# Cosine attention with a highway layer: k scaled ahead of the product, transfers over 128 lanes

## The chip, the cores and the metric

The kernel runs on one core of a Trainium2 chip. The metric is the device time of one execution in microseconds. The core has a matrix engine (TensorE, PE in the profile; its weight loads are listed apart as PEld), three engines for element-wise work (VectorE or DVE, ScalarE or ACT, GpSimd or POOL), and SyncE (SP), which here only issues transfers. Every engine works through its own list of instructions in order, and semaphores hold an instruction back until what it needs is there. Transfers are issued from SP, ACT and POOL and run on the core's 16 DMA engines.

## The reference

Eight batches b of 12 heads, 448 positions and 64 numbers a head; q, k and v are float32. Then a gated layer on all 3584 rows of 768 numbers:

```python
def _attn_ref(q, k, v, tau):                 # (8, 12, 448, 64), tau = 0.1
    q_n = q / (np.linalg.norm(q, axis=-1, keepdims=True) + 1e-06)
    k_n = k / (np.linalg.norm(k, axis=-1, keepdims=True) + 1e-06)
    scores = np.matmul(q_n, k_n.transpose(0, 1, 3, 2)) / tau
    scores = scores - np.max(scores, axis=-1, keepdims=True)
    attn = np.exp(scores)
    attn = attn / (np.sum(attn, axis=-1, keepdims=True) + 1e-09)
    return np.matmul(attn, v)

def _moe_ref(x, w_h, w_t, b_t):              # x: (3584, 768), weights 768 x 768
    H = np.maximum(x @ w_h, 0.0)
    T = 1.0 / (1.0 + np.exp(-(x @ w_t + b_t)))
    return T * H + (1.0 - T) * x
```

The rows of x are the positions of a batch, its columns the 12 heads side by side.

## The kernel before, in words

**Attention.** The heads of a batch go in six pairs p: head p in lanes 0 to 63 and head p + 6 in lanes 64 to 127 once they are transposed. A group g holds two pairs. Of the 448 keys of a head, 384 are three blocks c of 128; the last 64 keys of both heads of a pair make one more block, the tail ("t" in names). For each batch the kernel does the following:

- Squares on ACT (L353 q, L376 k, L387 k's tail, L373 k of batch 0), sums over 64 numbers on DVE (L361, L382, L389), and seven small steps of Newton's method on DVE (L401 to L408) that turn a sum of squares n into 1/sqrt(n), held in y. The factor 1/tau is folded into the norm of q.
- Scaling of q by its own y (L419), one multiplication of 128x448 for each of two halves t and three groups. It runs on POOL, but for one of batch 0 on DVE.
- k is not scaled. DVE copies it into pair order as float16 (kc, L471; for batch 0 the casts ck, L465), and POOL casts its tail (kb, L479).
- Transposes on PE with an identity as the moving operand (q: L431; k: L450 and L452), and copies out of PSUM on DVE (qT: L436, kT: L458).
- Scores on PE (L508, L519), 448 queries wide. Six exponentials of a pair on ACT (L514) and one of the tail (L521) write E and Et as float16; the scale of the exponential is y of the key, one number a lane. No maximum is subtracted: a cosine over tau is at most 10.
- Products with v on PE (L533, L538, L546); a column of ones in v gives the sum of the exponentials. DVE takes its reciprocal (L553) and scales (L554) into x.

**The gated layer.** The rows of a batch are cut into four parts i, numbered g = 4b + i; three have 128 rows (two rows j of each of 64 lanes) and the fourth has 64. PE transposes x (L577), DVE copies (L579), PE multiplies with wt and wh (L593, L590), DVE adds the bias into z (L602), ACT takes a tanh with the constant scale 0.5 (L609), DVE makes the gate (L611), relu(H) - x (L605) and their product hm (L614), POOL adds x (L619) into one of four output buffers os, and SP stores it (L628; the fourth part L626).

**Transfers.** SP loads q, the tails of k and v, and the bias, and stores. POOL loads k, v and the weights with a cast to float16. ACT issues three loads at the start. q of a batch is loaded as two transfers of 64 lanes, s = 0 and 1 (L284, L287); an output of 128 rows is stored as two transfers of 64 lanes, h = 0 and 1.

**Order.** The order is written out. Every operation has a number, in the order in which the Python code names it, and ORDER is a permutation of all 1,879 numbers. Each engine gets its instructions in that order. SLOTS says for each tile which of its ring's buffers it uses. Nothing is planned when the kernel is built. A change of the operations so comes with a new ORDER and new SLOTS.

Of the kernel before, what the change touches and what calls it, by code (L numbers as in the profile page):

```python
# [92 lines left out]
""".split()  # L93
)

SLOTS = {
    "qr": "01010101",
    "kr": "0120120",
    "kt": "01010010",
    "kb": "01010101",  # L100
    "kp": "01010101",
    "vr": "01010101",
    "vt": "01010110",
    "vp": "01010101",
    "sq": "0120210120202120120120102120120120101102202101020",
# [89 lines left out]
def kernel(  # L195
# [436 lines left out]
    for b in range(B):  # L632
        if b == 0:
# [5 lines left out]
            for p in range(2, 6):  # L639
                ld_k0(p, "SP")  # L640
# [97 lines left out]
```

## Time and profile before

| what | value |
|---|---|
| median of 3 runs | 289.96 us (289.58 to 292.29) |
| the profiled execution | 289.78 us, of which the profile's span is 288.0 |
| granted TensorE clock | 0.995 |
| busy: PE / DVE / ACT / POOL | 255.9 / 241.1 / 242.5 / 130.3 us |
| exponentials (L514, L521) | 336 instructions, 195.1 us busy |
| moved by DMA | 38.63 MB in 51,251 packets |
| of this SP's queue (q1) | 26.35 MB in 24,976 packets |

Instructions of one engine overlap: the next starts before the last has ended. So a group's busy time divided by its count is longer than the distance of two starts, and the distance is what an instruction costs in a full queue. A "DMA share" is the mean busy share of the 16 DMA engines; packets of several queues can overlap on one engine, so a share over 1 is possible. Idle time of an engine is put down to what ended it.

### The profile page before, as it was taken

The numbers are of one execution on the slowest core, as the hardware profiler recorded it, in microseconds if no ns is written. First come the engines' busy times: TensorE is split into PE (matmuls) and PEld (weight loads), VectorE is DVE, ScalarE is ACT, GpSimd is POOL, SyncE is SP. The second block draws the span as 40 slices with busy tenths as digits, with TensorE's granted clock in tenths as the row PEclk, the third lists the DMA queues.
The fourth block names the chain that finished last, engine by engine and source line by source line (L and its number), as shares of the span: only waits on it lengthen the run. The fifth ranks groups of instructions, "written<-read, shape, count | busy, mean of one in ns | idle before, by whom it ended". The sixth has DMA issues, their size and how long they took to land.

```text
span 288.0 us, 7655 instructions
## 1 busy us (share of the span) xinstructions
PE 255.9 (89%) x3024; PEld 160.7 (56%) x3024; DVE 241.1 (84%) x544; ACT 242.5 (84%) x421; POOL 130.3 (45%) x166
## 2 busy tenths in 40 slices
PE   0156899999999999999999999999999999999991
PEld 0122556655655656565756575665755576656650
DVE  2896895479999899999979999799999878565994
ACT  3378999999799989999999997989999787894220
POOL 1659048113574629034945168070764091206260
PEclk9999999999999999999999999999999999999997
DMA  7999999999498696822879917758004606000636
GB/s 174 231 218 227 258 236 204 231 196 141 56 102 146 113 226 186 180 68 35 108 141 238 145 31 192 165 81 168 2 3 112 81 3 192 2 2 2 191 88 185
DMA packets 51251, 38.63 MB, mean 134 GB/s; under 512 B 37648, under 2 KB 48016, under 8 KB 51216
## 3 DMA queue, kind: packets, MB, share of 16 engines
q1 hardware_dynamic: 24976, 26.35, 38.4%
q0 software_dynamic: 24896, 11.21, 31.6%
q10 hardware_dynamic: 1344, 0.59, 1.0%
q8 instruction: 23, 0.38, 0.5%
q14 instruction: 12, 0.10, 0.1%
HBM read 38.34 MB, written 11.01 MB: 171 GB/s over the span
## 4 chain that ended last, share of the span: by engine, by line
PE 38%; ACT 35%; DMA 8%; DVE 8%; issue 4%; SPq 2%; POOL 2%; POOLq 0%; ACTq 0%; DVEq 0%
ACT E L514 25%; PE B L593 15%; PE B L508 5%; PE B L538 5%; DMA qr<-in_q_dram 5%; ACT Et L521 5%; PE B L590 3%; DMA kt<-in_k_dram 2%; PE B L546 2%; ACT sq L353 2%; ACT tt L609 2%; POOL os L619 2%; PE B L533 2%; PE B L431 2%; PE B L577 1%
## 5 line engine op out<-in xcount | busy, mean ns | idle before, releaser
L514 ACT ACTIVATE E<-B,y 128x448 f16<-128x448 f32 x288 | 163.2, 690 | 12.3 <-PE B L508 12.0
L619 POOL TENSOR_TENSOR os<-x,hm 128x384 f32<-128x384 f16 x53 | 48.6, 929 | 87.3 <-DVE hm L614 60.6
L593 PEld LDWEIGHTS <-xT 128*128 128x128 f16 x576 | 52.1, 97 | 36.6 <-issue 7.6
L419 POOL TENSOR_TENSOR qn<-qr,y 128x448 f16<-128x448 f32 x47 | 44.3, 960 | 49.8 <-DVE y L408 30.7
L593 PE MATMUL B<-wt,xT 128*128 128x384 f16 x288 | 57.6, 326 | 0.7 <-DVE xT L579 0.3
L593 PE MATMUL B<-wh,xT 128*128 128x384 f16 x288 | 57.3, 326 | 0.8 <-ACT E L514 0.3
L508 PE MATMUL B<-qT,kT 64*128 64x448 f16 x288 | 49.3, 369 | 6.6 <-ACT Et L521 2.3
L538 PE MATMUL B<-vp,E 128*128 128x65 f16 x864 | 44.9, 194 | 0.1
L538 PEld LDWEIGHTS <-E 128*128 128x128 f16 x864 | 39.1, 98 | 4.0 <-issue 0.4
L609 ACT ACTIVATE tt<-z 128x768 f16<-128x768 f32 (+1 forms) x32 | 25.4, 798 | 16.9 <-DVE z L602 16.9
L605 DVE SCALAR_TENSOR_TENSOR hm<-B,x 128x384 f16<-128x384 f32 x56 | 29.9, 547 | 5.8 <-PE B L593 3.7
L533 PE MATMUL B<-vp,Et 128*128 128x130 f16 x144 | 32.3, 224 | 0.5 <-ACT Et L521 0.2
L602 DVE TENSOR_TENSOR z<-B,bias 128x384 f32<-128x384 f32 x48 | 26.1, 548 | 7.5 <-PE B L593 4.7
L521 ACT ACTIVATE Et<-B,y 128x448 f16<-128x448 f32 x48 | 31.9, 686 | 0.1
L554 DVE SCALAR_TENSOR_TENSOR x<-B,rd 128x448 f16<-128x448 f32 x48 | 29.3, 617 | 0.8
L361 DVE TENSOR_REDUCE n<-sq 128x14 f32<-128x896 f32 (+1 forms) x25 | 25.7, 1034 | 0.9 <-ACT sq L353 0.9
L353 ACT ACTIVATE sq<-qr 128x896 f32<-128x896 f32 (+1 forms) x24 | 23.3, 977 | 3.1 <-DMA qr<-in_q_dram 3.1
L508 PEld LDWEIGHTS <-kT 64*128 64x128 f16 x288 | 11.9, 95 | 25.0 <-issue 16.0
L450 PE MATMUL B<-ident,kp 128*128 128x128 f16 x144 | 14.7, 230 | 11.1 <-POOL ident masks.py:199 10.1
L382 DVE TENSOR_REDUCE n<-sq 128x18 f32<-128x1152 f32 (+2 forms) x17 | 21.5, 1270 | 0.8 <-ACT sq L376 0.8
L450 PEld LDWEIGHTS <-kp 128*128 128x128 f16 x144 | 10.5, 101 | 16.8 <-issue 10.0
L458 DVE COPY kT<-B 128x1024 f16<-128x1024 f16 (+1 forms) x27 | 16.6, 619 | 2.8 <-PE B L452 2.8
(53 smaller groups left out, 356.4 us busy)
## 6 DMA issues: line engine op xcount, KB each, us to landing
qr<-in_q_dram SPq DMA_DIRECT2D x14, 672.0 KB, 9.2
out_dram<-os SPq DMA_DIRECT2D x48, 192.0 KB, 3.1
kr<-in_k_dram POOLq DMA_DIRECT2D x7, 576.0 KB, 9.7
vr<-in_v_dram POOLq DMA_DIRECT2D x7, 576.0 KB, 8.8
vt<-in_v_dram SPq DMA_DIRECT2D x16, 96.0 KB, 7.4
out_dram<-os SPq DMA_DIRECT2D x16, 96.0 KB, 2.3
qr<-in_q_dram SPq DMA_DIRECT2D x6, 224.0 KB, 5.3
kt<-in_k_dram SPq DMA_DIRECT2D x14, 96.0 KB, 7.4
```

What stands on the lines that cost most here:

```text
L353: nc.scalar.activation(dst(), src(), AF.Square, scale=tau)
L419: ENG[eng].tensor_mul(R("qn", 3 * b + g)[:, :, t, :], R("qr", b)[:, g + 3 * t, :].rearrange("l (j d) -> l j d", d=D), R("y", b)[:, c : c + ...
L508: nc.tensor.matmul(R("B", ("S", n, c, t))[:, 0:S], lhsT=R("kT", i)[ln, s, 128 * c : 128 * c + 128], rhs=R("qT", i)[ln, s, :], start=True, ...
L514: nc.scalar.activation(R("E", n)[:, at : at + 7, :].rearrange("l j x -> l (j x)"), R("B", ("S", n, c, t))[:, 0:S], AF.Exp, scale=R("y", b) ...
L521: op("ACT", f"expt {n}", lambda: nc.scalar.activation(R("Et", n).rearrange("l j x -> l (j x)"), R("B", ("St", n))[:, 0:S], AF.Exp, scale=R ...
L533: nc.tensor.matmul(U[:, 2 * c : 2 * c + 2, :], lhsT=Et[:, 2 * c : 2 * c + 2, :].rearrange("l j x -> l (j x)"), rhs=vp[:, 6:8, 0:65], start ...
L538: nc.tensor.matmul(U[:, 2 * c + t, :], lhsT=E[:, at : at + 2, :].rearrange("l j x -> l (j x)"), rhs=vp[:, 3 * t + m, 0:65], start=False, s ...
L554: op("DVE", f"ev {n}", lambda: nc.vector.scalar_tensor_tensor(out=R("x", b)[:, :, D * p : D * p + D], in0=U_()[:, :, 0:D], scalar=0.0, in1 ...
L593: nc.tensor.matmul(P[:, 0:MH], lhsT=xT[:, cc, :], rhs=w_[:, cc, MH * mh : MH * mh + MH], start=(cc == 0), stop=(cc == CC - 1))
L605: op("DVE", f"hm {g} {mh}", lambda at=at, sl=sl, mh=mh: nc.vector.scalar_tensor_tensor(out=R("hm", g)[:, sl], in0=R("B", at)[:, 0:MH], sca ...
L609: op("ACT", f"th{nb} {g}", lambda: nc.scalar.activation(R("tt", g)[:, 0:W], R("z", g)[:, 0:W], AF.Tanh, scale=0.5), r=[("z", g)], w=[("tt" ...
L619: op(eng, f"out {g} {mh}", lambda sl=sl, mh=mh: ENG[eng].tensor_add(R("os", g)[:, sl], xpart(mh), R("hm", g)[:, sl]), r=[("gg", g), ("x", ...
```

## The change

- k is multiplied by its own y before it is transposed (scale_k, "kn"): one multiplication of 128x384 a pair, on DVE for the first two pairs of batch 0 and on POOL for the other 46. They take the place of the copies kc and the casts ck. The cast of k's tail becomes a multiplication too (scale_kb). The buffer kp now holds one pair and has six places.
- The exponentials have no scale from y any more.
- k's transposes of a group go into one PSUM tile; for batch 0 they come in three operations, with three copies.
- q of a batch, or a group of it in batch 0, is one transfer of 128 lanes, and so is the store of an output of 128 rows. The fourth part of a batch is stored as before.
- 18 products of zeros, 128x128 by 128x512, run on PE before its first real work.
- In batch 0 the loads of k and of its tail, but for the first, are issued by SP, and the norms of the first q and k share one Newton chain.
- ORDER and SLOTS are new. Among SP's instructions the first store stood behind the first half of q's load of batch 4, and now stands ahead of that load.

```diff
+    WARM = 18
-        kp=(2, [128, NP, NC, 2, D], FP16),
+        kp=(6, [128, NC, 2, D], FP16),
+    op("DVE", "zw", zero("DVE", [(wz[:, :], 0.0)]), w=[("wz",)])
+    for i in range(WARM):
+        op("PE", f"wm {i}", lambda i=i: nc.tensor.matmul(R("B", ("W", i))[:, :], lhsT=wz[:, 0:128], rhs=wz[:, 128:640],
+                                                         start=True, stop=True), r=[("wz",)], w=[("B", ("W", i)), ("wm",)], mode="F")
-    def q_src(b, s):
-        return q[b].rearrange("(u s) (l j) d -> s l u (j d)", s=2, j=NJ)[s]
+    def q_src(b):
+        return q[b].rearrange("(u s) (l j) d -> s l u (j d)", s=2, j=NJ)
...
-        for s in range(2):
-            def fn(s=s):
-                d, a = R("qr", b)[64 * s : 64 * s + 64], q_src(b, s)
...
+        def fn():
+            d, a = R("qr", b), q_src(b)
+            if len(gs) == 3:
+                ENG[eng].dma_start(d[:, :, :], a)
...
+    def kcol(b, p):
+        return R("y", b)[:, KCS[b > 0][0][p] : KCS[b > 0][0][p] + 6].rearrange("l (t c) -> l t c", t=2).unsqueeze(3).to_broadcast([128, 2, NC, D])
...
+    def scale_k(b, p, eng):
+        def fn():
+            if b == 0:
+                a = R("os", ("f0", p // 2)).rearrange("l (i h c d) -> l i h c d", i=2, h=2, c=NC)[:, p % 2]
+            else:
+                a = R("kr", b)[:, p::6, :].rearrange("l h (c d) -> l h c d", c=NC)
+            ENG[eng].tensor_mul(R("kp", 6 * b + p).rearrange("l c t d -> l t c d"), a, kcol(b, p))
...
-                ENG[eng].tensor_copy(R("kb", b)[ln, :, ab, :], R("kt", b)[ln, :, :])
+                ENG[eng].tensor_mul(R("kb", b)[ln, :, ab, :], R("kt", b)[ln, :, :],
+                                    R("y", b)[ln, c : c + 6].unsqueeze(2).to_broadcast([64, NP, D]))
...
-                                         AF.Exp, scale=R("y", b)[:, col : col + 1])
+                                         AF.Exp)
...
-            for h in range(2):
-                if tail:
+            if tail:
+                for h in range(2):
                     nc.sync.dma_start(rows[6, :, MH * h : MH * h + MH], O[64 * h : 64 * h + 64, 0:MH])
-                else:
-                    nc.sync.dma_start(rows[2 * i + h], O[64 * h : 64 * h + 64, :])
+            else:
+                nc.sync.dma_start(rows[2 * i : 2 * i + 2], O[:, :])
```

More of the change, by code (lines that the diff above doesn't have):

```diff
@@ L98 @@
     "kr": "0120120",
-    "kt": "01010010",
+    "kt": "01010101",
     "kb": "01010101",
-    "kp": "01010101",
+    "kp": "012345102345012345012345012345021345021345021435",
     "vr": "01010101",
-    "vt": "01010110",
+    "vt": "01010010",
     "vp": "01010101",
-    "sq": "0120210120202120120120102120120120101102202101020",
+    "sq": "0121012012012012012012101201212120120201201210211",
     "n2": "01010101",
     "y": "01201201",
-    "tu": "0110100101010",
+    "tu": "010101010101",
     "qn": "012012012012012012012012",
@@ new lines @@
+    "z": "01010101010101010010101010011010",
+    "tt": "01010110010110100101100101100101",
+    "hm": "01201021012010210201210120101201",
+    "os": "01230123212032030103021031303102310",
+    "B": (
+        "0123456701234567012456701347036512602371065021403450146234671350264371632047236450123740612736025743"
+        "1204573516372450130264731657240315035103521074503624735370462140563175406175203461753753146201736107"
+        "5234057642130542160574362513650274607267014325615261432065370624306574120712347605641340715260431524"
+        "7253627104527630254163410653217402712470631246071352130436714250361745304703516402761254607327465203"
+        "1546123567421362047260752414076542076351023174503720614537247325410623745103762401765367254176215604"
+        "1376410753620136725430215346126703517015436702531426714507361235467013475026714307162457130264"
@@ L279, in ld_q @@
     def ld_q(b, gs=range(3), eng="SP"):
-        for s in range(2):
-            def fn(s=s):
-                d, a = R("qr", b)[64 * s : 64 * s + 64], q_src(b, s)
-                if len(gs) == 3:
-                    ENG[eng].dma_start(d, a)
-                else:
-                    g = gs[0]
-                    ENG[eng].dma_start(d[:, g::3, :], a[:, g::3, :])
-            op(eng, f"ldq {b} {gs[0]} {s}", fn, w=[("qr", b, g) for g in gs])
+        def fn():
[3 more added lines that the diff above has]
+            else:
+                ENG[eng].dma_start(d[:, gs[0] :: 3, :], a[:, :, gs[0] :: 3, :])
+        op(eng, f"ldq {b} {gs[0]}", fn, w=[("qr", b, g) for g in gs])
     def ld_k0(p, eng):
@@ L437, in turn_q, with turn_k @@
             op("DVE", f"cpq{parts} {b} {g} {s}", cp, r=[("B", ("Tq", i))], w=[("qT", i, s)] if s is not None else [("qT", i, 0), ("qT", i, 1)])
-    def turn_k(b, g, joint):
+    def turn_k(b, g):
         i = 3 * b + g
-        for s in (None,) if joint else range(2):
-            at = ("Tk", i, s)
-            ss = range(2) if joint else (s,)
-            def fn(at=at, ss=ss):
-                T = R16(at)
-                for n, s in enumerate(ss):
-                    p = 2 * g + s
-                    for c in range(NC):
-                        nc.tensor.transpose(T[:, 512 * n + 128 * c : 512 * n + 128 * c + 128],
-                                            R("kp", b)[:, p, c].rearrange("l t d -> l (t d)"), ident[:, :])
-                    nc.tensor.transpose(T[:, 512 * n + 384 : 512 * n + 512],
-                                        R("kb", b)[:, p].rearrange("l ab d -> l (ab d)"), ident[:, :])
-            op("PE", f"tk{len(ss)} {b} {g} {s}", fn, r=[("kp", b, 2 * g + s_) for s_ in ss] + [("kb", b), ("id",)],
-               w=[("B", at)], mode="F")
-            def cp(at=at, ss=ss):
-                nc.vector.tensor_copy(R("kT", i)[:, ss[0] : ss[-1] + 1].rearrange("p s x -> p (s x)"), R16(at)[:, 0 : 512 * len(ss)])
-            op("DVE", f"cpk{len(ss)} {b} {g} {s}", cp, r=[("B", at)], w=[("kT", i, s_) for s_ in ss])
@@ L461, in cast_k0 @@
-    def cast_k0(p, eng):
-        def fn():
-            a = R("os", ("f0", p // 2)).rearrange("l (i h x) -> l i h x", i=2, h=2)[:, p % 2]
-            a, d = a.rearrange("l h (c d) -> l h c d", c=NC), R("kp", 0)[:, p].rearrange("l c t d -> l t c d")
-            ENG[eng].copy(d, a) if eng == "ACT" else ENG[eng].tensor_copy(d, a)
-        op(eng, f"ck {p}", fn, r=[("os", ("f0", p // 2), p)], w=[("kp", 0, p)])
-    def copy_k(b):
-        for t in range(2):
-            def fn(t=t):
-                nc.vector.tensor_copy(R("kp", b).rearrange("l p c t d -> l (p c) t d")[:, :, t],
-                                      R("kr", b)[:, 6 * t : 6 * t + 6, :].rearrange("l p (c d) -> l (p c) d", c=NC))
-            op("DVE", f"kc {b} {t}", fn, r=[("kr", b, p) for p in range(NP)], w=[("kp", b, p) for p in range(NP)])
@@ L475, in cast_kb, with part, tails @@
-    def cast_kb(b, eng):
+        at = ("Tk", i)
+        def part(s):
+            for c in range(NC):
+                nc.tensor.transpose(R16(at)[:, 512 * s + 128 * c : 512 * s + 128 * c + 128],
+                                    R("kp", 6 * b + 2 * g + s).rearrange("l c t d -> l c (t d)")[:, c], ident[:, :])
+        def tails():
+            for s in range(2):
+                nc.tensor.transpose(R16(at)[:, 512 * s + 384 : 512 * s + 512],
+                                    R("kb", b)[:, 2 * g + s].rearrange("l ab d -> l (ab d)"), ident[:, :])
@@ new lines, in copy @@
+        def copy(lo, n):
+            d = R("kT", i)
+            if lo == 0:
+                nc.vector.tensor_copy(d.rearrange("p s x -> p (s x)")[:, :], R16(at)[:, :])
+            elif n == 384:
+                nc.vector.tensor_copy(d[:, (lo - 1) // 2, 0:384], R16(at)[:, 256 * (lo - 1) : 256 * (lo - 1) + 384])
+            else:
+                nc.vector.tensor_copy(d[:, :, 384:512], R16(at).rearrange("p (s x) -> p s x", s=2)[:, :, 384:512])
+        if b > 0:
+            op("PE", f"tk8 {b} {g}", lambda: (part(0), part(1), tails()),
+               r=[("kp", 6 * b + 2 * g), ("kp", 6 * b + 2 * g + 1), ("kb", b), ("id",)], w=[("B", at)], mode="F")
+            op("DVE", f"cpk1024 {b} {g}", lambda: copy(0, 1024), r=[("B", at)], w=[("kT", i, 0), ("kT", i, 1), ("kT", i, "t")])
+            return
@@ new lines, in turn_k @@
+        for s in range(2):
+            op("PE", f"tk3 {b} {g} {s}", lambda s=s: part(s), r=[("kp", 6 * b + 2 * g + s), ("id",)] + ([("wm",)] if g == 0 and s == 0 else []),
+               w=[("B", ("Tk", i), s)], mode="F")
+            op("DVE", f"cpk384 {b} {g} {s}", lambda s=s: copy(1 + 2 * s, 384), r=[("B", at, s)], w=[("kT", i, s)])
+        op("PE", f"tk2 {b} {g}", tails, r=[("kb", b), ("id",)], w=[("B", ("Tk", i), "t")], mode="F")
+        op("DVE", f"cpk256 {b} {g}", lambda: copy(1, 256), r=[("B", at, "t")], w=[("kT", i, "t")])
@@ L502, in scores @@
         n = 6 * b + p
-        KC, KT = KCS[b > 0]
         for c in range(NC):
@@ L512, in fe @@
                 def fe(c=c, t=t):
-                    at, col = 7 * (2 * c + t), KC[p] + 3 * t + c
+                    at = 7 * (2 * c + t)
                     nc.scalar.activation(R("E", n)[:, at : at + 7, :].rearrange("l j x -> l (j x)"), R("B", ("S", n, c, t))[:, 0:S],
-                                         AF.Exp, scale=R("y", b)[:, col : col + 1])
-                op("ACT", f"exp {n} {c} {t}", fe, r=[("B", ("S", n, c, t)), ("y", b, "k", p)], w=[("E", n)])
+                                         AF.Exp)
+                op("ACT", f"exp {n} {c} {t}", fe, r=[("B", ("S", n, c, t))], w=[("E", n)])
         def ft():
             nc.tensor.matmul(R("B", ("St", n))[:, 0:S], lhsT=R("kT", i)[:, s, 384:512], rhs=R("qT", i)[:, s, :], start=True, stop=True)
-        op("PE", f"qkt {n}", ft, r=[("qT", i, s), ("kT", i, s)], w=[("B", ("St", n))], mode="F")
+        op("PE", f"qkt {n}", ft, r=[("qT", i, s), ("kT", i, "t")], w=[("B", ("St", n))], mode="F")
         op("ACT", f"expt {n}", lambda: nc.scalar.activation(
-            R("Et", n).rearrange("l j x -> l (j x)"), R("B", ("St", n))[:, 0:S], AF.Exp,
-            scale=R("y", b)[:, KT + p : KT + p + 1]), r=[("B", ("St", n)), ("y", b, "t")], w=[("Et", n)])
+            R("Et", n).rearrange("l j x -> l (j x)"), R("B", ("St", n))[:, 0:S], AF.Exp),
+           r=[("B", ("St", n))], w=[("Et", n)])
     def attend(b, p):
@@ L635 @@
             ld_k0(0, "ACT")
-            ld_kt(0, "ACT")
-            ld_k0(1, "ACT")
+            ld_kt(0, "SP")
+            for p in range(1, 6):
+                ld_k0(p, "SP")
             ld_q(0, [1], "SP")
-            for p in range(2, 6):
-                ld_k0(p, "SP")
             ld_q(0, [2], "SP")
@@ L659 @@
             newton(0, 66, 84, [("k", 3), ("k", 4), ("k", 5)])
-            for p in range(NP):
-                cast_k0(p, "DVE")
         else:
@@ L679 @@
                 newton(b, 0, 84, [("q", g) for g in range(3)] + [("k", p) for p in range(6)] + [("t",)])
-            copy_k(b)
-        cast_kb(b, "POOL")
+        scale_kb(b, "POOL")
         if b == 0:
@@ L690 @@
             scale_q(b, g, ("DVE", "POOL") if first else ("POOL", "POOL"))
+            for s in range(2):
+                scale_k(b, 2 * g + s, "DVE" if first else "POOL")
             turn_q(b, g, 2 if first else 1)
-            turn_k(b, g, b > 0)
+            turn_k(b, g)
         for p in range(NP):
```

39 lines of the change are left out of this document (16 added, 23 removed), and 145 rows, old and new, of the table ORDER.

## The prediction

> **What bounds the kernel now.** I read the head of the page first, then busy time by stage, then single rows of ACT for the spacing of its instructions, then the transfers, since the change touches all of these.
>
> From the page (busy time; DMA queue 1; the chain that ended last; groups):
>
> ```profile
> PE 255.9 (89%) x3024; PEld 160.7 (56%) x3024; DVE 241.1 (84%) x544; ACT 242.5 (84%) x421; POOL 130.3 (45%) x166
> ...
> q1 hardware_dynamic: 24976, 26.35, 38.4%
> ...
> PE 38%; ACT 35%; DMA 8%; DVE 8%; issue 4%; SPq 2%; POOL 2%; POOLq 0%; ACTq 0%; DVEq 0%
> ...
> L514 ACT ACTIVATE E<-B,y 128x448 f16<-128x448 f32 x288 | 163.2, 690 | 12.3 <-PE B L508 12.0
> L619 POOL TENSOR_TENSOR os<-x,hm 128x384 f32<-128x384 f16 x53 | 48.6, 929 | 87.3 <-DVE hm L614 60.6
> ...
> L419 POOL TENSOR_TENSOR qn<-qr,y 128x448 f16<-128x448 f32 x47 | 44.3, 960 | 49.8 <-DVE y L408 30.7
> ...
> out_dram<-os SPq DMA_DIRECT2D x48, 192.0 KB, 3.1
> ```
>
> Three engines are nearly full and the chain changes between PE and ACT. By stage (columns: stage, its length, then busy us of PE, PEld, DVE, ACT, POOL, each with its count, then the granted clock, DMA share, GB/s):
>
> ```profile
> 60.00:100.00 40.00, 39.15 (x427) 23.48 (x426) 37.90 (x76) 38.21 (x64) 21.34 (x25) 1.00 0.88 120
> 100.00:140.00 40.00, 38.81 (x501) 24.62 (x500) 38.09 (x83) 38.89 (x69) 17.27 (x20) 1.00 0.71 141
> 140.00:180.00 40.00, 39.24 (x496) 25.30 (x493) 37.30 (x80) 37.41 (x66) 23.21 (x27) 1.00 0.77 141
> ```
>
> In the middle ACT is idle 1 to 3 of 40 us and DVE 2 to 3; POOL has half its time free. No single engine can be relieved alone for more than a few per cent. Now ACT's rows in order of time:
>
> ```profile
> 39.93 5.88 ACT L514 ACTIVATE E<-B,y 128x448 f16<-128x448 f32 x11
> 45.62 0.71 ACT L521 ACTIVATE Et<-B,y 128x448 f16<-128x448 f32 x1
> ...
> 97.72 0.98 ACT L609 ACTIVATE tt<-z 128x768 f16<-128x768 f32 x1
> 98.45 0.77 ACT L521 ACTIVATE Et<-B,y 128x448 f16<-128x448 f32 x1
> 98.97 1.31 ACT L376 ACTIVATE sq<-kr 128x1152 f32<-128x1152 f16 x1
> 100.02 1.31 ACT L514 ACTIVATE E<-B,y 128x448 f16<-128x448 f32 x2
> ```
>
> Starts, not durations, give the price of an instruction in a full queue: eleven exponentials take 45.62 - 39.93 = 5.69 us, 0.517 each; the tanh with a constant scale over 768 columns takes 0.73, the square over 1152 takes 1.05. The last two give 0.32 / 384 = 0.83 ns a column and 0.09 us fixed.
>
> The SP queue:
>
> ```profile
> SPq L628 <- POOL os L619: 104.5, 11, 23.0
> ...
> 92.36 8.21 SPq L628 DMA_DIRECT2D out_dram<-os  x4
> ```
>
> The first store leaves at 92.36 us, and SP spends 104.5 us waiting for outputs to store: today neither its issue time nor the 3.1 us landing of a store is on the path.
>
> **The change part by part.**
>
> *Constant scale in the exponentials.* By the line above, 448 columns with a constant scale would take 0.09 + 0.37 = 0.46 us against 0.517. Times 336 (288 + 48) that is 19 us less on ACT; at the other end 0, if the spacing belongs to reading PSUM. I take 19, since both constant-scale rows lie on the line. The Trainium skill, "ScalarE: Activation LUTs", section "What ACT_TABLE_LOAD costs", prices one [128,1] pointer operand at about 93 ns; by it the sum would be 31 us, where these rows bear out about 60 ns each. DVE and PE are then late next: DVE sheds the copies of k (L471, 14 of 551 ns, 7.7 us) and the casts (L465, 6 of 494 ns, 3.0), and gains two scalings (1.2) and a few smaller copies of kT, about 9 us net. I count 11 us of gain on the path, with 0 and 19 as ends.
>
> *k scaled on POOL.* 46 multiplications of 128x384. The trace has none; the nearest rows are L419 (960 ns for 448 columns, 0.82 us scaled) and L619 (0.93 us for 384): 38 to 43 us. The 16 casts of k's tail become two-input products, 0.54 to about 0.82 us: 4 us. POOL goes from 130 to about 175 of 288 us. Cover: its idle time ahead of L619 and L419, 87.3 + 49.8 us. The new wait is k's transposes for POOL; behind them on PE stand the scores, and ACT waits for those. PE waits today 7 us in all for q's scaling; I take 0 more for k's, between 0 and 20 (a wait of up to 10 us for hm stands ahead of a scaling in POOL's queue, twice over the run).
>
> *q as one transfer, stores as one.* SP issues 10 loads of q in place of 20 and 24 stores in place of 48: 34 issues of 0.6 us off a queue that waits 104.5 us; 0 on the path, but 1 us at the start, where eight issues stand ahead of a q load in the chain. Before, the first store stood behind a load of q (batch 4) that waits for its buffer; in the new order it stands ahead of it, so it leaves when its last sum on POOL is done: 77.9 us in the trace, less 4 for faster exponentials, 74 us.
>
> What matters is the shape of the new store. q's load stays 128 x 6 x 448 on both sides, as its two strides run into one. The store's output does not: two rows j of a group lie 768 elements apart and the 64 lanes 5376, so the changed program carries 2 x 64 x 768 against 128 x 768. Its outermost count falls from 64 to 2. How are transfers dealt to the sixteen DMA engines? The trace answers for the old ones. SP's 121 issues carry 23,040 pieces (for instance 48 stores x 64, 14 loads of q x 64 x 6); the page counts 24,976 packets, and 24,976 - 23,040 = 1,936 = 121 x 16, one closing packet for every engine and issue. All those have outermost counts of 64 or 128 and inner ones of 1 to 6. An issue of 64 pieces (store) and one of 384 (q) take the same 0.60 and 0.62 us, so SP hands over a shape, not a list of pieces. A shape is cut along a dimension, and with the inner counts at 2, 3 or 6 the only one that gave sixteen parts was the outermost. With an outermost count of 2 that leaves **two engines**. No row shows such a case; the other end is sixteen, as now.
>
> The Trainium skill says the same for this case: "DMA: Bandwidth & Descriptors", section "Why a DMA increments its semaphore by 16 and not by 1", takes the largest number up to 16 that divides the slowest dimension of both sides, and on SP's queue always the lowest-numbered engines. By it the 24 stores all use the same two. The trace agrees for 64 and 128; for 2 no run here shows it.
>
> Price: a store is 128 pieces of 3,072 bytes. The trace's quicker half of such packets took 121 to 134 ns, so 64 in a row take 7.7 us on an engine, against some 1.5 us today. The stage from 279.50 to 286.00, mostly stores, moves 199 GB/s at a DMA share of 0.72, 17.3 GB/s an engine or 11.4 us a store: the upper end, as sixteen engines then disturb each other. I take 7.7: 24 x 7.7 = 186 us on each of the two engines. After 74 us they also carry their sixteenth of the rest: about 27 us of SP's own packets, in line behind the stores, and 37 of POOL's loads (packets at their quickest, 18 to 74 ns and 49 ns). Queues overlap on an engine, since the DMA share reaches 1.26 in one stage; I count half of POOL's, 19.
>
> Sum: 74 + 186 + 27 + 19 = 306. The pair is not always fed (four output buffers; loads wait behind stores), 10 us; the profiled execution lies 1.8 us over its span, 289.78 against 288.0, and 0.2 under the median of 289.96: 318, say **320 us**. Some 230 us of work for the pair stand behind the first store, so a shorter compute is worth nothing there. Without the 10 and with POOL's loads wholly hidden: 289. At 11.4 us a store: 24 x 3.7 = 89 more, over 400, which I hold for unlikely, since two engines alone do not fill the memory; 134 ns gives 20 more.
>
> *Zero products first.* Seven transposes took 0.93 us at 13.56 us and 0.50 at 109 us, so PE starts at half speed while the page's clock says 1.00; each further 128 columns cost 0.12 us. The 18 products of 512 columns, 0.47 us each at that rate, wait only for a memset on DVE (0.22 us in its row), start at about 2 us and end by about 10, where PE does its first work today (10.14, waiting for ident). At most 2 us of that lies on the path, before the first exponentials; 0 counted. The new order itself I count at 0, within 4 either way.
>
> **The rivals.**
>
> *Sixteen engines after all: faster.* If a transfer is dealt by pieces (128 divides by 16 as well), the store costs what it does today. Then 290 - 11 - 1 = 278 us (270 to 284). For it: every issue so far closes on sixteen. Against: the constant cost of an issue. It decides at the closing packets of 24 stores.
>
> *Sixteen engines, and POOL becomes the bound.* POOL runs in order, sums that wait for hm stand ahead of k's scalings, and PE would wait for them in each of 24 groups: 278 plus 0.6 x 24 = 292 (285 to 300). For it: POOL doubles its work per group of q and k; against: 87 us of idle time.
>
> **How the numbers follow.** Two engines: 0.80, 320 us, its own range 294 to 372. Sixteen and faster: 0.14. Sixteen with a late POOL: 0.06. I lean to the first because the rows leave no other dimension by which sixteen parts were cut, though they leave a cut by pieces possible. The range 290 to 372 holds the first and half of the third. 1% (2.9 us) is about what a measurement of this kernel can tell from no change. Faster by over 1%: 0.14; within 1%: 0.04; slower: 0.82.
>
> **What would show it.** Queue 1 should count 24 x (16 - 2) = 336 closing packets fewer than sixteen an issue would give; the landing of a store should rise from 3.1 us to 10 and more; queues of stores should run on after the last product; and ACT, DVE and PE should each show more idle time from 75 us on. Exponentials should start 0.46 us apart. Wrong I am if the store lands in 3 to 4 us; then the time is that of a rival, and POOL's waits tell which.

## The result, and the profile after

| what | before | after |
|---|---|---|
| median | 289.77 us of 4 runs (288.14 to 292.29) | 336.56 us of 4 runs (335.81 to 337.60) |
| ratio, 95% interval | | 1.161 (1.152 to 1.170) |
| profiled execution, its span | 289.78, 288.0 us | 336.25, 334.4 us |

The changed kernel is 16% slower. The forecast was 320 us, its range 290 to 372.

From the page after the change: busy time by engine, DMA queue 1, the chain that ended last by engine and by line, two groups, and the store.

```profile
PE 260.0 (78%) x3042; PEld 160.8 (48%) x3042; DVE 245.5 (73%) x523; ACT 215.4 (64%) x421; POOL 173.9 (52%) x212
...
q1 hardware_dynamic: 25168, 26.74, 26.0%
...
PE 32%; DVE 18%; DMA 15%; issue 12%; ACT 7%; POOL 5%; SPq 5%; DVEq 0%; POOLq 0%; ACTq 0%
DMA out_dram<-os 14%; PE B L610 13%; ACT E L531 5%; PE B L525 4%; SPq L308 3%; PE B L555 3%; DVE hm L631 2%; DVE hm L622 2%; PE B L607 2%; DVE n L391 2%; PE B L440 2%; PE B L536 2%; DVE x L571 2%; PE B L594 1%; PE B L454 1%
...
L531 ACT ACTIVATE E<-B 128x448 f16<-128x448 f32 x288 | 136.4, 568 | 27.0 <-PE B L525 16.6
...
L489 POOL TENSOR_TENSOR kp<-kr,y 128x384 f16<-128x384 f16 x42 | 35.5, 853 | 6.4 <-PE B L610 5.1
...
out_dram<-os SPq DMA_DIRECT2D x24, 384.0 KB
```

The chain went through PE and ACT before; now its longest line is the landing of stores. Queue 1 shows how the stores are dealt. SP's 90 issues carry 24,064 pieces of data; 25,168 - 24,064 = 1,104 closing packets, and 66 issues x 16 + 24 stores x 2 = 1,104. That is 336 fewer than sixteen an issue would give, the forecast's number: every single store goes to **two engines**. The packet records of the trace say the same: two store packets are on the way for 168 us, one for 23, more than two for 8, where the second run with stores in halves (below) has fifteen or more for 25 us. The page gives no landing time for these stores. In the packet records one that runs alone is on the way for 8 to 11 us; the first, issued at 62.2 us, ends at 74.4, so 12 us from issue to landing, against 3.1 before.

By stage (columns: stage, length, busy us of PE, PEld, DVE, ACT, POOL with counts, granted clock, DMA share, GB/s):

```profile
60.00:100.00 40.00, 36.96 (x441) 23.27 (x440) 38.29 (x77) 31.25 (x61) 23.26 (x27) 0.96 0.74 128
100.00:140.00 40.00, 37.32 (x512) 24.61 (x511) 37.74 (x74) 31.51 (x62) 30.32 (x37) 1.00 0.64 129
140.00:180.00 40.00, 30.91 (x374) 19.14 (x372) 28.89 (x62) 29.73 (x56) 18.40 (x22) 0.96 0.53 117
...
280.00:310.00 30.00, 12.79 (x96) 7.72 (x94) 12.57 (x26) 3.05 (x4) 7.12 (x8) 0.80 0.16 59
310.00:334.40 24.40, 0.00 (x0) 0.00 (x0) 2.42 (x6) 0.00 (x0) 0.00 (x0) 0.50 0.15 56
```

In the stage from 140 us every engine loses time. But the larger part comes at the end: by the trace PE's last product ends at 292.8 us, 11 us later than before (281.8), and what follows for 41 us is, but for a few last sums, stores, at 56 GB/s and a DMA share of 0.15, that is 2.4 of 16 engines.

Queue SP in order of time (start, us, instruction; a row of several issues runs from the first start to the last end and holds SP's waits between them):

```profile
62.19 0.65 SPq L645 DMA_DIRECT2D out_dram<-os  x1
...
116.74 6.60 SPq L291 DMA_DIRECT2D qr<-in_q_dram  x1
125.01 5.54 SPq L645 DMA_DIRECT2D out_dram<-os  x1
130.60 11.55 SPq L308 DMA_DIRECT2D kt<-in_k_dram  x2
142.26 0.58 SPq L645 DMA_DIRECT2D out_dram<-os  x1
142.88 10.96 SPq L314 DMA_DIRECT2D vt<-in_v_dram  x2
...
266.14 25.23 SPq L645 DMA_DIRECT2D out_dram<-os  x5
```

While a backlog stands on the two engines, the issue itself can be held: the load of q at 116.74 us takes 6.60 us to issue, a store at 125.01 takes 5.54, where such issues took about 0.6 before. Of the five stores at 266 us, by their single records, only the last was held, for 7.38 us; the rest of that row is waiting. And a load that is issued still has a part on the slow pair: of the 768 pieces of the q issued at 116.74, 672 land by 133 us and the other 96, two sixteenths, between 136 and 142 us, in a gap between two stores. So late stores make late loads. ACT shows what that leads to, and the new spacing of the exponentials (starts, as before):

```profile
118.41 2.76 ACT L531 ACTIVATE E<-B 128x448 f16<-128x448 f32 x6
120.97 1.20 ACT L538 ACTIVATE Et<-B 128x448 f16<-128x448 f32 x2
...
142.51 1.79 ACT L362 ACTIVATE sq<-qr 128x896 f32<-128x896 f32 x2 [5.58 <-DMA qr<-in_q_dram]
```

Six exponentials take 120.97 - 118.41 = 2.56 us, 0.427 each, where they took 0.517 (medians of all pairs that follow each other in the two traces: 0.424 and 0.516). And ACT waits 5.58 us for the q issued at 116.74, until its last pieces are there. The waits of POOL and of the SP queue (us in total, times, longest):

```profile
POOL os L636 <- DMA out_dram<-os: 51.8, 11, 7.0
...
SPq L645 <- POOL os L636: 72.6, 8, 21.9
```

The first is new: output buffers that a store has not left. The second says that SP also waits for outputs, so the pair of engines isn't always fed.

### The profile page after: what moved, and what is told of

Same layout as the page of the kernel before. It is cut to its first block, busy times and chain, and to the rows that moved or that the text cites. A ratio compares the mean times of both kernels' runs of the same rounds, so it can differ in the third digit from the quotient of the medians.

```text
span 334.4 us, 7654 instructions
## 1 busy us (share of the span) xinstructions
PE 260.0 (78%) x3042; PEld 160.8 (48%) x3042; DVE 245.5 (73%) x523; ACT 215.4 (64%) x421; POOL 173.9 (52%) x212
## 3 DMA queue, kind: packets, MB, share of 16 engines
q1 hardware_dynamic: 25168, 26.74, 26.0%
## 4 chain that ended last, share of the span: by engine, by line
PE 32%; DVE 18%; DMA 15%; issue 12%; ACT 7%; POOL 5%; SPq 5%; DVEq 0%; POOLq 0%; ACTq 0%
DMA out_dram<-os 14%; PE B L610 13%; ACT E L531 5%; PE B L525 4%; SPq L308 3%; PE B L555 3%; DVE hm L631 2%; DVE hm L622 2%; PE B L607 2%; DVE n L391 2%; PE B L440 2%; PE B L536 2%; DVE x L571 2%; PE B L594 1%; PE B L454 1%
## 5 line engine op out<-in xcount | busy, mean ns | idle before, releaser
L531 ACT ACTIVATE E<-B 128x448 f16<-128x448 f32 x288 | 136.4, 568 | 27.0 <-PE B L525 16.6
L636 POOL TENSOR_TENSOR os<-x,hm 128x384 f32<-128x384 f16 x53 | 48.2, 922 | 87.5 <-DMA out_dram<-os 51.8
L610 PE MATMUL B<-wt,xT 128*128 128x384 f16 x288 | 61.2, 338 | 6.2 <-ACT E L531 6.2
L610 PE MATMUL B<-wh,xT 128*128 128x384 f16 x288 | 59.7, 332 | 0.2 <-DVE xT L596 0.2
L428 POOL TENSOR_TENSOR qn<-qr,y 128x448 f16<-128x448 f32 x47 | 45.1, 967 | 12.8 <-issue 6.8
L525 PE MATMUL B<-qT,kT 64*128 64x448 f16 x288 | 44.3, 363 | 6.0 <-DVE kT L467 1.9
L489 POOL TENSOR_TENSOR kp<-kr,y 128x384 f16<-128x384 f16 x42 | 35.5, 853 | 6.4 <-PE B L610 5.1
L538 ACT ACTIVATE Et<-B 128x448 f16<-128x448 f32 x48 | 27.2, 575 | 6.5 <-PE B L536 6.4
L631 DVE TENSOR_TENSOR hm<-tt,hm 128x768 f16<-128x768 f16 (+1 forms) x32 | 24.0, 756 | 0.4
L496 POOL TENSOR_TENSOR kb<-kt,y 64x384 f16<-64x384 f32 x16 | 13.6, 849 | 20.0 <-DVE y L417 12.3
L536 PE MATMUL B<-qT,kT 128*128 128x448 f16 x48 | 17.9, 383 | 5.5 <-ACT E L531 2.9
```

The source lines that it names most:

```text
L428: ENG[eng].tensor_mul(R("qn", 3 * b + g)[:, :, t, :], R("qr", b)[:, g + 3 * t, :].rearrange("l (j d) -> l j d", d=D), R("y", b)[:, c : c + ...
L489: ENG[eng].tensor_mul(R("kp", 6 * b + p).rearrange("l c t d -> l t c d"), a, kcol(b, p))
L525: nc.tensor.matmul(R("B", ("S", n, c, t))[:, 0:S], lhsT=R("kT", i)[ln, s, 128 * c : 128 * c + 128], rhs=R("qT", i)[ln, s, :], start=True, ...
L531: nc.scalar.activation(R("E", n)[:, at : at + 7, :].rearrange("l j x -> l (j x)"), R("B", ("S", n, c, t))[:, 0:S], AF.Exp)
L610: nc.tensor.matmul(P[:, 0:MH], lhsT=xT[:, cc, :], rhs=w_[:, cc, MH * mh : MH * mh + MH], start=(cc == 0), stop=(cc == CC - 1))
L631: op("DVE", f"gg{nb} {g}", lambda: nc.vector.tensor_mul(R("hm", g)[:, 0:W], R("tt", g)[:, 0:W], R("hm", g)[:, 0:W]), r=[("gt", g), ("hm", ...
```

## The experiments

The theory: two engines a store are the loss, and the rest of the change alone is faster. The rival: the new order, or POOL's added work, costs the time and the slow stores only show it.

**Stores in two halves again, all else as changed.**

```diff
-                nc.sync.dma_start(rows[2 * i : 2 * i + 2], O[:, :])
+                for h in range(2):
+                    nc.sync.dma_start(rows[2 * i + h], O[64 * h : 64 * h + 64, :])
```

> The changed kernel with its 24 stores outside the tail issued as two halves of 64 lanes each, as in the kernel before; all else stays changed. Theory (two engines per single store are the whole loss): 336 to 272, between 266 and 280, and some 90 issues x 16 + 24 x 16 closing packets, 1,824, in place of 1,104 on queue 1; the landing back at 3 to 4 us. Rival (the loss is of the new order, or of POOL with k's scaling, and the slow stores only show it): still 290 or more. Half way (two terms): 280 to 290, and POOL then ends the longest waits of PE.

Measured: 284.83 us (282.99 to 285.64), ratio to the kernel before 0.981 (0.977 to 0.986). From its page:

```profile
q1 hardware_dynamic: 25888, 26.75, 34.6%
...
PE 62%; DVE 20%; issue 6%; ACT 4%; DMA 4%; POOL 1%; SPq 1%; DVEq 0%; ACTq 0%
...
out_dram<-os SPq DMA_DIRECT2D x48, 192.0 KB, 3.1
```

25,888 - 24,064 = 1,824 closing packets, as expected, and the landing is 3.1 us again. One edit of the store takes 51.7 us away (336.56 - 284.83) and leaves a kernel faster than the one before. But 285 is above 280, in the branch called half way: the rest of the change brings 5 us, not the 12 of the prediction. The sign named for that branch is not seen: PE's waits for k scaled on POOL come to 0.4 us in this run.

**Single stores alone, all else as before.**

```diff
-                    nc.sync.dma_start(rows[2 * i + h], O[64 * h : 64 * h + 64, :])
+                nc.sync.dma_start(rows[2 * i : 2 * i + 2], O[:, :])
```

> The kernel before with nothing changed but its 24 stores, each one transfer. Theory (two engines): the pair has 24 x 7.7 = 186 us of stores and some 45 us of other packets behind a first store at 92 us, so 92 + 231 + 2 = 325, between 305 and 340, and 24 x (2 x 16 - 2) = 720 fewer closing packets on queue 1 than the kernel before. Rival (single stores cost little in themselves, the order written for them matters): 288 to 294.

Measured: 347.61 us (346.42 to 348.03), ratio 1.198 (1.194 to 1.202). From its page, and its last stage:

```profile
q1 hardware_dynamic: 24256, 26.35, 30.1%
```

```profile
310.00:346.00 36.00, 0.00 (x0) 0.00 (x0) 5.74 (x12) 1.36 (x2) 2.13 (x3) 0.50 0.15 56
```

24,976 - 24,256 = 720 closing packets fewer, to the packet, and the same drain at 56 GB/s. So neither the new order nor POOL is needed for the loss. The time lies 8 us above the range, though: a store alone costs more than the sum of packets says. In its packet records the 24 stores are 197 us of work for each engine of the pair, not 186, and no store packet is on the way for 41 us after the first.

**Single stores on POOL's queue.**

```diff
-                nc.sync.dma_start(rows[2 * i : 2 * i + 2], O[:, :])
-        op("SP", f"st {g}", store, r=[("os", g)], w=[("o", g)])
+                nc.gpsimd.dma_start(rows[2 * i : 2 * i + 2], O[:, :])
+        op("SP" if tail else "POOL", f"st {g}", store, r=[("os", g)], w=[("o", g)])
```

> The changed kernel with the 24 single stores issued on POOL's queue in place of SP's; their shape is as in the changed kernel. Theory A (what costs is that every store goes to the same two engines): if the other queue deals each store to another pair, as the Trainium skill has it ('DMA: Bandwidth & Descriptors', section 'Why a DMA increments its semaphore by 16 and not by 1': a rotating start for fewer than sixteen), stores spread and the time falls to 275 to 300, the issues on POOL being the rest. Theory B (every queue takes the same lowest two): 330 to 345. Both say that one store lands in 8 us or more.

Measured: 369.10 us (367.83 to 369.70), ratio 1.272 (1.268 to 1.277): slower than both expectations. From its page, and its longest wait:

```profile
q0 software_dynamic: 37568, 20.73, 33.7%
q1 hardware_dynamic: 22048, 17.31, 18.1%
...
out_dram<-os POOLq DMA_DIRECT2D x24, 384.0 KB, 12.1
```

```profile
POOL os L636 <- DMA out_dram<-os: 90.1, 13, 11.2
```

Queue 1 loses 25,168 - 22,048 = 3,120 packets, 130 a store: 128 pieces and two closings, which confirms the count of two once more. On the other queue the stores do spread: the packet records show two large packets on the way at most times, but four or more for 45 us, which one pair can't carry; SP's stores in the changed kernel show more than two for 8 us only. That agrees with the rotating start that the Trainium skill gives for this queue ("DMA: Bandwidth & Descriptors", section "Why a DMA increments its semaphore by 16 and not by 1"). It helps nothing, because each store still lands in 12.1 us and POOL is now the one that waits: its sums stand, in one list with the stores, before buffers that only such a store can free. The run says that a rotating pair does not save this order; it can't say what it would save with stores that stand behind nothing.

**Eight output buffers in the changed kernel.**

```diff
-        os=(4, [128, DM], FP32), B=(8, [128, 512], FP32))
+        os=(8, [128, DM], FP32), B=(8, [128, 512], FP32))
...
+                    if t[0] == "os":
+                        free = [j for j in range(8) if ("os", j) not in held or left[held["os", j]] == 0]
+                        i = min(free, key=lambda j: last.get(("os", j), -1))
```

> The changed kernel, its single stores on SP as they are, with eight buffers of the output tile os in place of four. Theory (the rate of two engines: 24 stores of 8.4 us, which the trace shows, and some 46 us of other packets behind a first store at 62 us): the compute runs ahead, the stores do not; at most the gaps between stores go, 64 us less the 46 of other packets: 318 to 337. Rival (the stores only hold up the sums because four buffers are too few for a store that lands in 10 us): 284 to 300.

Measured: 332.68 us (331.47 to 333.93), ratio 1.149 (1.144 to 1.153), 3.9 us under the changed kernel. Its waits begin, and its last stage is:

```profile
POOL os L640 <- DVE hm L635: 55.3, 13, 12.1
```

```profile
300.00:330.00 30.00, 0.00 (x0) 0.00 (x0) 0.00 (x0) 0.00 (x0) 0.00 (x0) 0.50 0.15 55
```

POOL's 51.8 us of waiting for stores is gone and almost nothing comes of it. PE's last product ends at 288.6 us, 4 sooner than in the changed kernel, and for the last 30 us no engine has work but the transfers. The wait for buffers was a symptom. What is left is the rate of two engines, 193 us for the 24 stores, and 57 us after the first store in which no store packet is on the way.

**What a constant scale is worth.** Two runs: the one with stores in halves, its scale read from a column of ones; and the kernel before with a constant scale.

```diff
-                                         AF.Exp)
+                                         AF.Exp, scale=one[:, 0:1])
```

> The run with stores in two halves, with the scale of all 336 exponentials again read from a column of the chip's memory, here a column of ones; the values are the same. It measures what a constant scale is worth where the stores do not bind: ACT has 336 x 0.094 = 31.6 us more work by the spacing of the exponentials in the two profiles. Theory (ACT is on the path for about half of that): 10 to 20 us over the run with two halves. Rival 1 (ACT is off the path, PE and DVE bind): 0 to 5. Rival 2 (ACT binds throughout): 25 to 32.

Measured: 295.23 us (294.44 to 295.60), 10.4 over the run with halves, ratio to the kernel before 1.019 (1.015 to 1.022).

```diff
-                                         AF.Exp, scale=R("y", b)[:, col : col + 1])
+                                         AF.Exp, scale=0.125)
```

> The kernel before with its 336 exponentials scaled by the constant 0.125 in place of the column y; k's norms are computed as before and not used, so the output leaves out the scaling by k's norm. All waits stay. Theory (ACT and PE change places on the path; the run with pointers and halves lost 10.4): 277 to 282. Rival 1 (the old order was written around a slower ACT, so the gain is not taken): 286 to 291. Rival 2 (all of 31.6 us): 258 to 262.

Measured: 279.68 us (278.14 to 280.15), 10.9 under the kernel before's 290.54 in the same runs, ratio 0.962 (0.958 to 0.966). From its page, the chain and the exponentials:

```profile
PE 57%; DMA 19%; DVE 14%; issue 3%; POOL 2%; ACT 1%; SPq 1%; POOLq 0%; ACTq 0%; DVEq 0%
...
L514 ACT ACTIVATE E<-B 128x448 f16<-128x448 f32 x288 | 136.4, 564 | 23.2 <-PE B L508 21.6
```

In both orders, some 31 us less on ACT (336 x 0.092) give 10 to 11. ACT's share of the chain falls from 35% to 1% and PE's grows from 38% to 57%: PE, at 247 busy of 278 us, is what is late next. Set side by side, DVE's scalings into x in the two runs with halves drift apart over most of the run: the one with pointers is half a microsecond ahead at 30 us, 3 behind at 68, 10 at 192 and 11 at 255. The gain has no one place.

**POOL with next to no scaling of k.**

```diff
-            ENG[eng].tensor_mul(R("kp", 6 * b + p).rearrange("l c t d -> l t c d"), a, kcol(b, p))
+            N = D if eng == "DVE" else 8
+            ENG[eng].tensor_mul(R("kp", 6 * b + p).rearrange("l c t d -> l t c d")[:, :, :, 0:N], a[:, :, :, 0:N], kcol(b, p)[:, :, :, 0:N])
...
-                ENG[eng].tensor_mul(R("kb", b)[ln, :, ab, :], R("kt", b)[ln, :, :],
+                ENG[eng].tensor_mul(R("kb", b)[ln, :, ab, 0:8], R("kt", b)[ln, :, 0:8],
```

> The run with stores in two halves, with the scalings of k and of its tail on POOL cut to 8 of 64 features (the others stay zero, so most of k is left out); the instructions, their order and waits stay, POOL has some 30 us less work. It tells what POOL's part costs. Theory (POOL's scalings hide): 283 to 286, no gain against 284.8. Rival (late scalings hold up PE: 5.2 us that the changed kernel with pointers and halves is over the kernel before): 278 to 281.

Measured: 277.64 us (276.81 to 278.52), ratio 0.955 (0.951 to 0.960); that is 7.2 us under the run with halves, whose ratio is 0.981 (0.977 to 0.986). Its page:

```profile
PE 255.1 (92%) x3042; PEld 160.7 (58%) x3042; DVE 238.7 (86%) x527; ACT 215.1 (78%) x421; POOL 137.5 (50%) x212
```

PE is busy as long as in the first run with halves (254.4 us), in a span shorter by 4.4 us (276.7 against 281.1). Beside the second profile with halves (span 283.3), the exponentials lie within 1.2 us of each other to 100 us and then step apart, by 2 us at about 110, 2 at 205 and 2 at 211. The third step lies between the two profiles with halves as well, so it is not POOL's. The other two could come from k's scalings that stand late in POOL's queue, behind sums that wait for hm. In the first run with halves (us in total, times, longest):

```profile
POOL os L636 <- DVE hm L631: 39.0, 12, 7.6
PEld L454 <- POOL kp L489: 0.4, 1, 0.4
```

But the second row says that PE hardly waits for them. What differs at the two steps is DVE. First the second profile with halves, then the run with a light POOL, the same instructions in each:

```profile
102.19 2.95 DVE L631 TENSOR_TENSOR hm<-tt,hm 128x768 f16<-128x768 f16 x2
...
201.50 2.76 DVE L628 TENSOR_SCALAR tt<-tt 128x384 f16<-128x384 f16 x1
```

```profile
101.79 0.89 DVE L632 TENSOR_TENSOR hm<-tt,hm 128x768 f16<-128x768 f16 x2
...
199.31 0.25 DVE L629 TENSOR_SCALAR tt<-tt 128x384 f16<-128x384 f16 x1
```

The first pair loses 2.1 us, the second 2.5, and both rows of the slower run lie on a stretch in which POOL goes from one instruction to the next without a pause (at 201.50: a sum twice, then a scaling of q, to 204.15 us). Over the whole first run with halves, these two steps of DVE (L628, L631) take 0.43 us on average where POOL works for under a fifth of their time, and 1.02 where it works for over four fifths. DVE's work from PSUM does not change (hm<-B,x: 548 ns in both runs). In all, DVE is busy for 238.7 us here against 244.4 and 245.3 with halves. So in these two places what POOL's added work costs is DVE's time beside it, and not PE's waiting for k. How much of the 7.2 us this is in runs without a profile stays open.

**v's tail cast on ACT, to relieve POOL.**

```diff
-                ENG[eng].tensor_copy(R("vp", b)[ln, :, 6 + ab, 0:D], R("vt", b)[ln, :, :])
+                nc.scalar.copy(R("vp", b)[ln, :, 6 + ab, 0:D], R("vt", b)[ln, :, :])
...
-        cast_vt(b, "POOL")
+        cast_vt(b, "ACT")
```

> The run with stores in two halves, with the 16 casts of v's tail (0.5 us each) on ACT in place of POOL, where the scalings of k crowd. POOL has 8.7 us less work; 30 us less gave 7.2, so by proportion 2: 282 to 285. Rival (ACT's queue stands in front of the casts and holds up the products with v): 286 to 290.

Measured: 286.73 us (284.45 to 287.29), ratio 0.989 (0.985 to 0.992), against 284.97 beside it on the same chip. Nothing gained. The median is in the range of the rival, 1.8 us over the run beside it, but single executions of the two overlap (282.90 to 286.13 beside 284.45 to 287.29), and whether ACT's queue holds the casts up was not measured. Taking 8.7 us off POOL in this way brings nothing.

**q in halves again, and zero products of 8 columns.** Both start from the run with stores in halves.

```diff
-            if len(gs) == 3:
-                ENG[eng].dma_start(d[:, :, :], a)
...
+            for s in range(2):
+                if len(gs) == 3:
+                    ENG[eng].dma_start(d[64 * s : 64 * s + 64, :, :], a[s])
```

> The run with stores in two halves, with each load of q in two halves of 64 lanes as well: 10 issues more on SP. Theory (SP's issue time is off the path but for the start): within 1 us of the run with stores in two halves (284.8). Rival (a single transfer of q loads slower or faster in itself): 3 us or more away from it.

Measured: 288.62 us (285.38 to 289.75), ratio 0.991 (0.987 to 0.995). The two that were to be compared were measured on different chips, so both were run again side by side on one.

> The run with stores in two halves once more, so that it stands beside the run with q in halves on one chip: 283 to 286.

> Stores and loads of q in two halves, once more. If q's single transfer gains nothing: within 1 us of the run beside it. If the difference of the first two (3.8 us, from two calls) is real: 3 to 4 us over it.

Measured: stores in halves 284.97 us (282.90 to 286.13), ratio 0.984 (0.980 to 0.988); q in halves as well 289.24 us (286.35 to 291.07), ratio 0.997 (0.993 to 1.000). The difference of some 4 us is real. SP's queue with q whole, and then with q in halves:

```profile
4.36 1.58 SPq L293 DMA_DIRECT2D qr<-in_q_dram  x2
5.99 1.28 SPq L314 DMA_DIRECT2D vt<-in_v_dram  x2
7.31 1.97 SPq L299 DMA_DIRECT2D os<-in_k_dram  x2
```

```profile
5.23 2.66 SPq L294 DMA_DIRECT2D qr<-in_q_dram  x4
7.93 1.71 SPq L315 DMA_DIRECT2D vt<-in_v_dram  x2
10.63 1.12 SPq L300 DMA_DIRECT2D os<-in_k_dram  x2
```

And ACT's first exponentials, in the same order:

```profile
15.86 3.60 ACT L531 ACTIVATE E<-B 128x448 f16<-128x448 f32 x8
```

```profile
20.01 3.57 ACT L532 ACTIVATE E<-B 128x448 f16<-128x448 f32 x8
```

k's last two loads of batch 0 leave 3.3 us later, the first exponentials come 4.2 us later, and the last ones still are 4.2 us late. Issue time of 0.6 us each is not all of it. By the trace's records in the run with q in halves SP starts seven issues in a row, the two of k among them, 17 ns after the load eight issues ahead of each has landed (k's at 10.63 after 10.61 us and at 11.37 after 11.36). So in this kernel SP waits for the eighth issue back, and loads in halves put k's two further back in that line.

```diff
-        op("PE", f"wm {i}", lambda i=i: nc.tensor.matmul(R("B", ("W", i))[:, :], lhsT=wz[:, 0:128], rhs=wz[:, 128:640],
+        op("PE", f"wm {i}", lambda i=i: nc.tensor.matmul(R("B", ("W", i))[:, 0:8], lhsT=wz[:, 0:128], rhs=wz[:, 128:136],
```

> The run with stores in two halves, with the 18 zero products of 8 columns in place of 512, so that PE has next to no work before the first transposes. Theory of the prediction (at most 2 us on the path): 284 to 288, and PE's first transposes again at 0.9 us for seven. Rival (in the profiles the granted clock of the first 40 us is 0.80 with the zero products and 1.00 in the kernel before, so they spend a budget that PE wants later): 280 to 284, with the clock of the first 40 us back near 1.00.

Measured: 285.29 us (284.88 to 285.55), ratio 0.983 (0.980 to 0.986): no difference. PE's first real work with products of 512 columns (the changed kernel), and of 8:

```profile
10.24 0.56 PE L440 MATMUL B<-ident,qn 128*128 128x128 f16 x7 [2.91 <-POOL qn L428]
...
15.05 0.74 PE L525 MATMUL B<-qT,kT 64*128 64x448 f16 x6 [0.45 <-DVE kT L467]
```

```profile
10.06 0.93 PE L440 MATMUL B<-ident,qn 128*128 128x128 f16 x7 [7.16 <-POOL qn L428]
...
14.73 1.30 PE L525 MATMUL B<-qT,kT 64*128 64x448 f16 x6 [0.71 <-DVE kT L467]
```

The zero products do what they can, seven transposes in 0.56 us in place of 0.93 and six scores in 0.74 in place of 1.30, and the 0.9 us do not reach the end. The granted clock of the first 40 us reads 0.81 with them (in the second run with halves) and 1.00 without; the rival, that this costs time later, is not borne out either.

## Why the prediction was right, and where its terms were off

**Two engines** carried it. The dealing of the stores, read from a count of closing packets that showed sixteen for outermost counts of 64 and 128, came out to the packet in every run that changed a store. The rule of the Trainium skill that was set beside it ("DMA: Bandwidth & Descriptors", section "Why a DMA increments its semaphore by 16 and not by 1") agrees. Of the marks named, the 336 packets, the drain after the last product and the idle engines are in the profile after; the landing shows only in packet records, and the spacing came out smaller, 0.42 us for 0.46.

**The sum**, 318 us, was made of a first store at 74, 186 of stores, 46 of other packets, 10 not fed and 1.8 outside the span. The profile has 62.2, 192 (64 pieces at a mean of 125 ns rather than 121, 24 times), 80 for the rest, and 1.8. So two terms were off in opposite directions, and that the sum still came within 17 us of the time is in part luck:

- The first store was put at 74 us, 77.9 less a gain of 4 for faster exponentials. It left at 62.2. The run with halves and pointers, in the same order, issues its first store at 65.0, those with halves at 62.7 and 63.1, those with q in halves as well at 64.1 and 65.9: so the exponentials give about 2 us and q's single loads 1 to 3. The other 10 or so fall to the rest of the change, the new order among it, which was counted as 0; no run parts them.
- "The pair is not always fed", 10 us, is the step that failed in size. No store packet is on the way for 67 us after the first; other packets, counted as 46, can fill only part of that. The cause named was right, loads behind stores and four buffers, but the price was not worked out. The buffers are 4 us of it, by the run with eight. The loads are seen in SP's rows and in the packets (a load of q held for 6.6 us, its last two sixteenths behind two stores, then ACT without work for 5.6), but were not separated by a run of their own, so how the rest is shared stays open.

The upper price, 11.4 us a store as in a stage in which sixteen engines disturb each other, was rightly left aside: the pair took 8.0 us a store.

**The constant scale** was priced at 0.057 us an exponential (19 us by 336) from a tanh and a square that read SBUF; it is 0.092 (median spacing 0.516 to 0.424). The 93 ns of the Trainium skill ("ScalarE: Activation LUTs", section "What ACT_TABLE_LOAD costs") agree with that, and the nearest rows missed it. Their line gives 0.46 us for a constant scale, which is 0.04 too much for the exponentials; that these read PSUM may be why, but no run shows it. ACT so loses some 31 us, not 19. On the path 11 were counted and 10.4 and 10.9 measured. Both numbers hold together because PE binds sooner than the step assumed. That none of it counts in the changed kernel, as the prediction says, was not measured by itself.

**POOL.** The scaling takes 0.85 us (0.82 to 0.93 was said), the tail's 0.85 (0.82), and POOL is busy 173.9 us (175). On the path it was put at 0, between 0 and 20: it is about 7, by the run without it. So the size lies in the range, but the way in is not the one named. With stores in halves, PE's waits for k's scaling come to 0.4 us; what the rows show instead is DVE's 16-bit steps drawn out beside a busy POOL, 4 us at the two steps, a term that the prediction does not have.

**q** was put at 1 us; it is about 4. The place was right (SP's issues at the start), but what stands in line behind is k's loads, held by 3.3 us, not only one load of q, and they wait for landings as well as for issue time. **Zero products** at 0 are right, the faster start included. **The new order** at 0 within 4: 290.0 - 10.4 - 4 + 7.2 = 282.8, and 284.9 is measured with halves, so 2 us are left for it and for the changed copies of k, no more than the terms can be off.

**The rivals.** With sixteen engines the kernel takes 284.9, between the 278 and the 292 given, since POOL's added work costs half of the 14 us that the second of them has. Both fell by the dealing of the stores, as was said.

## What to carry to other kernels

A transfer that is made simpler in the code can be dealt to fewer DMA engines: look at the outermost count of the shape that both sides share, and count closing packets in the profile. Where a store is slow, ask for what stands behind it in its queue; more buffers do not help much if the transfer's own rate binds. An engine with idle time is not free either: ask whose work runs beside it. And take the changes apart: here stores in two halves with the rest of the change run at 285.0 us, 1.6% to 1.9% under the kernel before and 15% under the changed one, the fastest complete kernel of this study.

## What the runs showed of the hardware that was not expected

- The time of an issue on SP's queue is not constant. With stores queued on two engines many single issues took 2 to 9 us (a load of q 6.60, one of v's tail 9.26, a store 7.38). In the kernel before most took 0.4 to 0.8 us, none more than 1.6 from the first store on, but one 4.7 earlier, behind loads of q and of k's tail.
- A load that is dealt to sixteen engines is late when two of them are: 672 of 768 pieces of a q landed by 133 us, the last 96, two sixteenths, between 136 and 142.
- DVE's 16-bit work from and to SBUF can be drawn out beside a busy POOL: 128x384 took 2.76 us there and 0.25 with POOL idle.
- The same store is cut differently by queue. On SP's it is 128 pieces of 3,072 bytes and 2 closings. On POOL's it is 528 packets by the page's counts (12,672 more for 24 stores), in the packet records 64 of 6,144 bytes (234 ns each), 448 of 8 bytes and 16 closings.
- The granted clock of the record can stand at 1.00 while PE takes 0.93 us for its first seven transposes, and at 0.84 (9 to 12 us, changed kernel) while it takes 0.56 us for them.
